# Attention scores on VectorE and ScalarE: one product per key unit, sums shared by two engines

## The chip, the cores and the metric

One core of a Trainium2 chip runs the whole program in one launch. The metric is the device time in microseconds; the kernel before has a median of 1359.05 us over three runs (1358.47 to 1362.22).

## The reference

Two equal layers in float32, for two sequences with one query token each. A layer is an attention block over a given cache and a gated feed-forward block, both with a LayerNorm ahead and a residual around:

```
x = x + A(layernorm(x)) ; x = x + B(layernorm(x))          # twice, with the same weights
A: q = x @ wq                    B=2, H=16 heads, Dh=256
   p = softmax(q . k_cache / 16) Sk=4096 keys for each head and sequence
   o = p @ v_cache, then o @ wo
B: h = relu(x @ W_gate) * (x @ W_up) ; h @ W_down          D=448, F=1792
```

The two caches are 2 x 16 x 4096 x 256 floats each, 134 MB a piece, and both layers read both of them.

## The kernel before

The caches go through SBUF in units. A unit is 1 MB: 128 partitions with 8 tiles (CT) of 256 floats (DH) each, so 1024 keys. One head of one sequence (a pair) is four units of K and four of V, and a layer has 32 pairs, which the text numbers u = 0 to 31. All loads are issued by SyncE (SP) at line 118, in an order fixed in advance: K of u, V of u - 1, after every odd u the head's weights (wq and wo, 896 KB), K of u + 1 and so on, at the end seven loads of W_gate and W_up (`w_in`) and four of W_down (`w_out`). Most K and V loads take four units in one transfer of 4 MB. The first thirteen loads of the second layer and the last twelve of each layer are single units.

The arena has room for 27 units: six blocks of four and three singles. A load is issued when the slot that it takes has been released (`release`, `pump`), and loads leave strictly in order. K of u + 3 takes the slots of K of u, so that its load waits for the scores of u; V goes likewise by the weighing.

The second layer goes through the pairs in reverse. The last pairs' units of the first layer stay in the arena for it (`keep`, `KEPT`): K of the second layer's u = 0, 1 and 2, V of its u = 0 and 1 and one unit of V of u = 2. While the feed-forward block runs between the layers, only what the few free slots hold can be loaded: K units 0 to 2 of u = 3 and two heads' weights. All later loads wait for scores: K unit 3 of u = 3 and the three V units of u = 2 take the slots of K of u = 0, the four K units of u = 4 those of K of u = 1, V of u = 3 the block of V of u = 0, and K of u = 5 the block of K of u = 2.

The function `score(u, c)` (lines 329 to 341) takes one K unit. For each of its eight tiles one VectorE instruction (line 336) multiplies the tile with the query, which stands alike in all 128 partitions, and sums the 256 products into one column of `s_of[u]`. The products are written over the tile, or into `junk` where the unit is kept for the second layer. The loop at line 433 sets the order of each engine's work for a pair u: unit 0 of the scores, `out_add` and `out_turn` for u - 2, units 1 and 2, `out_keep` and `project` for u - 2, in odd u `query` for the next head, `softmax_sum` for u - 1, unit 3, `softmax_max` and `softmax_exp` for u, then `weigh` for u - 1 on TensorE and `out_copy` for u - 1 on ScalarE. ScalarE's own work for a pair is small: the copy of the query (line 311, in odd u), two activations for the softmax (352 and 355) and the copy of the weighed sum (386). The schedule is written by hand; each engine executes its instructions in this order.

Of the kernel before, what the change touches and what calls it, by code (L numbers as in the profile page):

```python
# [9 lines left out]
AF = mybir.ActivationFunctionType  # L10
ALU = mybir.AluOpType
AX = mybir.AxisListType
RED = bass_isa.ReduceOp

B, D, H, S, DH, F = 2, 448, 16, 4096, 256, 1792
P = 128
# [3 lines left out]
CT = 8  # L20
# [5 lines left out]
SUMS = 96  # L26
SMALL = 13
ENDS = 12
HEAD = FULL * DH + P + 2 * D
EPS = 1e-5  # L30
SCALE = DH**-0.5
# [33 lines left out]
def two_layers(  # L65
# [10 lines left out]
    nc = tc.nc  # L76
# [45 lines left out]
    def get(*key):  # L122
        at = at_of[key]
        return arena[:, at * UNIT : (at + 1) * UNIT]

    def release(*key):
        units.free.add(at_of.pop(key))
        pump()
# [19 lines left out]
    def grouped(keys, begin, end):  # L148

        keys = list(keys)  # L150
        found, i = [], 0
        while i < len(keys):
            kind, name, c = keys[i]
            whole = kind in "kv" and c == 0 and begin <= i and i + NC <= len(keys) - end
            found.append((keys[i], NC if whole else 1))
            i += found[-1][1]
        return found
# [10 lines left out]
    of_second[NC - 1 : NC - 1] = heads  # L168
    pending += grouped(of_first, 0, ENDS) + [(key, 1) for key in ffn_loads]
    pending += grouped(of_second, SMALL, ENDS) + [(key, 1) for key in ffn_loads]  # L170

    row = consts.tile([P, 2 * DH], F32, name="row")
    junk = consts.tile([P, DH], F32, name="junk")
# [83 lines left out]
    def attention(order, after, begun):  # L257
# [4 lines left out]
        q_of, oT_of, s_of, mx_of, p_of, r_of, po_of, pT_of = ({} for _ in range(8))  # L262
# [3 lines left out]
        def query_of(u, pq):  # L266
            h, b = order[u]
            w = get("h", h, 0)
            for c in range(FULL):
                nc.tensor.matmul(  # L270
                    pq[:, b, :],
                    xT[:, c, b : b + 1].to_broadcast([P, P]),
                    w[:, c * DH : (c + 1) * DH],
                    start=(c == 0),
                    stop=False,
                )
            for j in range(2):
                nc.tensor.matmul(
                    pq[:, b, j * P : (j + 1) * P],
                    xT[:, FULL + j, b : b + 1].to_broadcast([P, P]),  # L280
                    w[:, FULL * DH : FULL * DH + P],
                    start=False,
                    stop=(j == 1),
                )
            q_of[u] = pq[:, b, :]
# [31 lines left out]
        def first_query():  # L317
# [3 lines left out]
            w = get("h", order[0][0], 0)  # L321
            for u, at in ((0, HEAD), (1, 0)):
                query_of(u, pq)
# [5 lines left out]
        def score(u, c):  # L329
            kt = get("k", order[u], c).rearrange("p (t n) -> p t n", t=CT)  # L330
            if c == 0:
                s_of[u] = work.tile([P, NT], F32, name="scores")
            kept = ("k", order[u], c) in after
            for t in range(CT):
                n = c * CT + t
                nc.vector.scalar_tensor_tensor(  # L336
                    junk if kept else kt[:, t, :], kt[:, t, :], 1.0, q_of[u],
                    op0=ALU.mult, op1=ALU.mult, accum_out=s_of[u][:, n : n + 1],
                )
            if not kept:  # L340
                release("k", order[u], c)

# [87 lines left out]
        ahead = 2 if ("k", order[0], 0) in keep else 0  # L430
        if ahead:
            query(ahead)
        for u in range(n_u + 2):
            if_pair(score, u, 0)
            if u == 0:
                inverse()
                nc.vector.tensor_scalar_mul(sr, rstd, SCALE)
                nc.vector.tensor_scalar_mul(nsr, rstd, -SCALE)
            if_pair(out_add, u - 2)
            if_pair(out_turn, u - 2)  # L440
            if_pair(score, u, 1)
            if_pair(score, u, 2)
            if_pair(out_keep, u - 2)
            if_pair(project, u - 2)
            if u % 2 and ahead < u + 1 < n_u:
                query(u + 1)
            if_pair(softmax_sum, u - 1)
            if_pair(score, u, 3)
            if_pair(softmax_max, u)
            if_pair(softmax_exp, u)  # L450
            for c in range(NC):
                if_pair(weigh, u - 1, c)
            if_pair(out_copy, u - 1)
# [87 lines left out]
    found = row[SUMS : SUMS + B, :D]  # L541
# [53 lines left out]
```

## Time and profile before

| | us |
|---|---|
| median of three runs | 1359.05 |
| the profiled execution, its own time | 1361.46 |
| its span in the profile | 1359.7 |
| VectorE busy | 796.3 (59%) |
| TensorE matmuls busy | 583.0 (43%) |
| ScalarE busy | 106.9 (8%) |

The profile is of one execution. It gives each engine's busy time, the share of time in which the core's 16 DMA engines were busy with the rate in GB/s, and chains of waits. Queue q1 carries the loads of SyncE. The queues q8 and q14 carry instructions, which the engines fetch while they run. The span falls into a first layer (to about 690 us), a stretch between the layers in which the load rate drops, and the second layer.

### The profile page before, as it was taken

Reading aid. Unit: us, or ns where it says so; the run is one execution under the profiler, and the core shown is the slowest. Engines: PE = TensorE matmul, PEld = TensorE weight load, DVE = VectorE, ACT = ScalarE, POOL = GpSimd, SP = SyncE. Lnnn points to the kernel's source line nnn. Section 1 sums busy time; section 2 is a strip of 40 time slices with the busy share of each in tenths; the row PEclk is TensorE's granted clock in tenths of the full one; section 3 lists DMA queues with packets and bytes.
Section 4 is the critical chain, followed back from the end, with each engine's and each line's share of the span. In section 5 each row is a group of like instructions: output and inputs, shape, how many; then the busy total and the mean of one; then the engine's idle time right before and its main releaser. Section 6 shows DMA issues by size and latency. Waiting matters only on the chain.

```text
span 1359.7 us, 11857 instructions
## 1 busy us (share of the span) xinstructions
PE 583.0 (43%) x3046; PEld 190.0 (14%) x3046; DVE 796.3 (59%) x4484; ACT 106.9 (8%) x314; POOL 76.6 (6%) x192
## 2 busy tenths in 40 slices
PE   2334335344244342443575444444244343443446
PEld 2111111111011110112131111111011110111112
DVE  4764664645646556466619984655646557456471
ACT  1100000000000000000011100000000000000001
POOL 0100000000000000000000100000000000000000
PEclk9666576666666756767676777666666665666667
DMA  9999999999999999999869999999999999999995
GB/s 397 438 427 429 432 428 431 431 430 431 429 429 431 429 434 430 429 428 425 328 259 370 417 433 431 430 428 428 431 428 436 434 427 427 431 429 433 425 416 194
DMA packets 29163, 563.33 MB, mean 414 GB/s; under 512 B 3236, under 2 KB 3240, under 8 KB 10024
## 3 DMA queue, kind: packets, MB, share of 16 engines
q1 hardware_dynamic: 29092, 562.58, 97.5%
q8 instruction: 24, 0.39, 0.1%
q14 instruction: 43, 0.35, 0.1%
q10 hardware_dynamic: 4, 0.00, 0.0%
HBM read 562.56 MB, written 0.00 MB: 414 GB/s over the span
## 4 chain that ended last, share of the span: by engine, by line
DVE 39%; DMA 34%; another core or an unknown queue 22%; PE 4%; issue 1%; ACT 0%; SPq 0%; DVEq 0%; POOL 0%; POOLq 0%; ACTq 0%
DVE arena L336 35%; DMA arena<-in_k_cache_dram 24%; DMA arena<-in_v_cache_dram 4%; DMA arena<-in_w_head_dram 3%; DMA arena<-in_w_in_dram 2%; DVE row L389 1%; DMA arena<-in_w_out_dram 1%; DVE ri L365 1%; PE po L375 1%; PE pf L518 1%; DVE mx L345 0%; PE acc L416 0%; PE pq L270 0%; PE pf L467 0%
## 5 line engine op out<-in xcount | busy, mean ns | idle before, releaser
L336 DVE SCALAR_TENSOR_TENSOR arena<-arena 128x256 f32<-128x256 f32 x1952 | 689.3, 421 | 453.6 <-DMA arena<-in_k_cache_dram 441.2
L375 PE MATMUL po<-arena,probs 128*2 128x512 f32 x2048 | 316.1, 764 | 176.2 <-DMA arena<-in_v_cache_dram 165.8
L397 PE MATMUL small<-ones,row 128*128 128x1 f32 x256 | 61.6, 344 | 369.5 <-DVE row L389 369.5
L336 DVE DVE_READ_ACCUMULATOR arena<-arena 128x1 f32 x1952 | 160.4, 82 | 0.0
L397 PEld LDWEIGHTS small<-ones,row 128*128 128x128 f32 x256 | 56.1, 305 | 431.6 <-DVE row L389 431.6
L416 PE MATMUL acc<-arena,oT 128*2 128x448 f32 x128 | 51.6, 905 | 142.1 <-DVE oT L406 142.1
L375 PEld LDWEIGHTS po<-arena,probs 128*2 128x2 f32 x2048 | 54.2, 98 | 388.4 <-issue 359.7
L299 PE MATMUL pq<-arena,xs 128*33 128x256 f32 x174 | 77.6, 616 | 60.3 <-DMA arena<-in_w_head_dram 60.3
L315 POOL PARTITION_BROADCAST arena<-arena x58 | 28.0, 552 | 635.6 <-ACT arena L311 623.5
L352 ACT ACTIVATE nm<-top,nsr 128x1 f32<-128x1 f32 x64 | 18.9, 295 | 528.5 <-POOL top L347 528.5
L347 POOL PARTITION_ALL_REDUCE top<-mx x64 | 24.5, 382 | 531.2 <-DVE mx L345 530.0
L311 ACT ACTIVATE arena<-pq 33x256 f32<-33x256 f32 x29 | 11.0, 378 | 515.7 <-PE pq L303 515.7
L389 DVE SCALAR_TENSOR_TENSOR row<-po,ri,row 128x256 f32<-128x256 f32 x64 | 30.7, 480 | 26.5 <-ACT row L386 26.4
L299 PEld LDWEIGHTS pq<-arena,xs 128*33 128x33 f32 x174 | 25.9, 165 | 130.7 <-issue 129.6
L386 ACT ACTIVATE row<-po,ri 128x256 f32<-128x256 f32 x64 | 30.2, 472 | 132.0 <-PE po L375 132.0
L336 DVE SCALAR_TENSOR_TENSOR junk<-arena,pq 128x256 f32<-128x256 f32 x64 | 26.9, 420 | 8.0 <-DMA arena<-in_k_cache_dram 6.0
L359 POOL PARTITION_ALL_REDUCE total<-rs x64 | 25.3, 395 | 64.3 <-ACT probs L355 64.3
L303 PE MATMUL pq<-arena,xs 128*33 128x128 f32 x116 | 28.3, 393 | 0.0
L355 ACT ACTIVATE probs<-scores,nm,sr 128x32 f32<-128x32 f32 x64 | 26.4, 413 | 2.1
L416 PEld LDWEIGHTS acc<-arena,oT 128*2 128x2 f32 x128 | 3.0, 82 | 144.8 <-DVE oT L406 144.8
L303 PEld LDWEIGHTS pq<-arena,xs 128*33 128x33 f32 x116 | 19.9, 171 | 15.3 <-issue 13.1
L467 PE MATMUL pf<-arena,xs 128*32 128x448 f32 x128 | 17.6, 698 | 3.1 <-DMA arena<-in_w_in_dram 2.3
(90 smaller groups left out, 187.6 us busy)
## 6 DMA issues: line engine op xcount, KB each, us to landing
arena<-in_k_cache_dram SPq DMA_DIRECT2D x57, 4096.0 KB, 50.4
arena<-in_v_cache_dram SPq DMA_DIRECT2D x57, 4096.0 KB, 54.3
arena<-in_w_head_dram SPq DMA_DIRECT2D x31, 896.0 KB, 43.2
arena<-in_v_cache_dram SPq DMA_DIRECT2D x19, 1024.0 KB, 21.0
arena<-in_k_cache_dram SPq DMA_DIRECT2D x16, 1024.0 KB, 25.4
arena<-in_w_in_dram SPq DMA_DIRECT2D x14, 896.0 KB, 18.3
arena<-in_w_out_dram SPq DMA_DIRECT2D x4, 896.0 KB, 16.7
arena<-in_w_out_dram SPq DMA_DIRECT2D x4, 672.0 KB, 9.9
```

The lines of the kernel that those rows point to most:

```text
L299: nc.tensor.matmul(q, xs[:, c, :], w[:, c * DH : (c + 1) * DH], start=(c == 0), stop=False)
L303: nc.tensor.matmul(q[:, j * P : (j + 1) * P], xs[:, FULL + j, :], w[:, FULL * DH : FULL * DH + P], start=False, stop=(j == 1),)
L315: nc.gpsimd.partition_broadcast(q_of[v], found[32 * b : 32 * b + 1], channels=P)
L336: nc.vector.scalar_tensor_tensor(junk if kept else kt[:, t, :], kt[:, t, :], 1.0, q_of[u], op0=ALU.mult, op1=ALU.mult, accum_out=s_of[u][: ...
L347: nc.gpsimd.partition_all_reduce(mx_of[u], mx, P, RED.max)
L355: nc.scalar.activation(p_of[u], s_of.pop(u), AF.Exp, bias=nm, scale=sr[:, b : b + 1], accum_out=rs)
L359: nc.gpsimd.partition_all_reduce(r_of[u], rs, P, RED.add)
L375: nc.tensor.matmul(po_of[u][32 * t : 32 * t + 2, :], p_of[u][:, n : n + 2], vt[:, 2 * t * DH : (2 * t + 2) * DH], start=(c == 0), stop=(c ...
L386: nc.scalar.activation(row[:, :DH], po_of[u][:, :DH], AF.Copy, scale=r_of[u][:, 0:1])
L389: nc.vector.scalar_tensor_tensor(row[:, :DH], po_of.pop(u)[:, DH:], r_of[u][:, 1:2], row[:, :DH], op0=ALU.mult, op1=ALU.add,)
L397: nc.tensor.matmul(pT_of[u][:, c : c + 1], row[:, c * P : (c + 1) * P], ones, start=True, stop=True,)
L416: nc.tensor.matmul(acc[at : at + B], oT_of[h][:, c, :], wo[:, c * D : (c + 1) * D], start=(n < 3), stop=(n >= n_u - 3),)
```

## The change

In `score`, units that are neither kept nor of the first two pairs of the first layer take another path. One `tensor_mul` multiplies the whole unit (2048 floats per partition) with the query, which is broadcast over the eight tiles. ScalarE then sums three tiles, each by an activation Copy with an accumulated output, and VectorE sums the other five by one `reduce_sum`. The products stand in place of the keys as before, and the unit is released when both engines are done. In the first layer this concerns 27 pairs (u = 2 to 28), in the second all 32. Everything else stays.

```diff
+BY_ACT = 3
...
-            for t in range(CT):
-                n = c * CT + t
-                nc.vector.scalar_tensor_tensor(
-                    junk if kept else kt[:, t, :], kt[:, t, :], 1.0, q_of[u],
-                    op0=ALU.mult, op1=ALU.mult, accum_out=s_of[u][:, n : n + 1],
-                )
+            found = s_of[u][:, c * CT : (c + 1) * CT]
+            if kept or ahead and u < ahead:
+                for t in range(CT):
+                    nc.vector.scalar_tensor_tensor(
+                        junk if kept else kt[:, t, :], kt[:, t, :], 1.0, q_of[u],
+                        op0=ALU.mult, op1=ALU.mult, accum_out=found[:, t : t + 1],
+                    )
+            else:
+
+                nc.vector.tensor_mul(kt, kt, q_of[u][:, None, :].to_broadcast([P, CT, DH]))
+                for t in range(BY_ACT):
+                    nc.scalar.activation(
+                        kt[:, t, :], kt[:, t, :], AF.Copy, accum_out=found[:, t : t + 1]
+                    )
+                nc.vector.reduce_sum(found[:, BY_ACT:], kt[:, BY_ACT:, :], axis=AX.X)
```

`ahead` is 2 in the first layer and 0 in the second.

## Rows read from the trace of the kernel before

**Rows 1.** The page, parts 1 to 3: engines, load rate, DMA queues.
```profile
PE 583.0 (43%) x3046; PEld 190.0 (14%) x3046; DVE 796.3 (59%) x4484; ACT 106.9 (8%) x314; POOL 76.6 (6%) x192
...
GB/s 397 438 427 429 432 428 431 431 430 431 429 429 431 429 434 430 429 428 425 328 259 370 417 433 431 430 428 428 431 428 436 434 427 427 431 429 433 425 416 194
...
q1 hardware_dynamic: 29092, 562.58, 97.5%
q8 instruction: 24, 0.39, 0.1%
q14 instruction: 43, 0.35, 0.1%
```

**Rows 2.** Stretches: busy us (instructions) by engine, last clock, DMA share, GB/s.
```profile
20.00:660.00 640.00, 260.72 (x1316) 85.33 (x1314) 385.22 (x2164) 47.70 (x142) 36.51 (x90) 0.65 1.00 429
676.00:688.00 12.00, 6.66 (x44) 3.29 (x48) 2.29 (x12) 2.39 (x4) 0.00 (x0) 0.84 0.08 35
750.00:752.00 2.00, 0.00 (x0) 0.00 (x0) 1.97 (x12) 0.68 (x3) 0.37 (x1) 1.00 0.65 279
752.00:1342.00 590.00, 250.15 (x1316) 77.58 (x1320) 352.81 (x2011) 44.89 (x137) 35.30 (x87) 0.66 1.00 427
1343.00:1354.00 11.00, 8.96 (x81) 2.75 (x73) 1.67 (x5) 1.13 (x4) 0.00 (x0) 1.00 0.07 28
```

**Rows 3.** Chain of waits through the layers' border: start, us, what.
```profile
658.97 20.86 DMA arena<-in_v_cache_dram
...
679.88 1.08 PE po L375 x8
...
714.80 2.85 DVE arena L336 x16
...
735.55 2.77 DVE arena L336 x16
```

**Rows 4.** Chain of waits at the end of the program.
```profile
1337.89 16.16 DMA arena<-in_w_out_dram
...
1354.10 0.99 PE pf L518 x6
```

**Rows 5.** SyncE's loads in order of issue, around the layers' border.
```profile
661.46 0.33 SPq L118 DMA_DIRECT2D arena<-in_w_in_dram  x1
...
664.11 8.74 SPq L118 DMA_DIRECT2D arena<-in_w_in_dram  x4
...
738.76 0.38 SPq L118 DMA_DIRECT2D arena<-in_v_cache_dram  x1
750.52 0.33 SPq L118 DMA_DIRECT2D arena<-in_k_cache_dram  x1
...
766.58 0.33 SPq L118 DMA_DIRECT2D arena<-in_k_cache_dram  x1
```

**Rows 6.** VectorE by line and shape: count, busy us, mean ns, idle before.
```profile
L336 DVE SCALAR_TENSOR_TENSOR arena<-arena 128x256 f32<-128x256 f32 x1952 | 689.3, 421 | 453.6 <-DMA arena<-in_k_cache_dram 441.2 <-ACT arena L324 7.6 <-POOL arena L315 4.7
L345 DVE TENSOR_REDUCE mx<-scores 128x1 f32<-128x32 f32 x64 | 11.9, 186 | 2.2
L490 DVE TENSOR_TENSOR row<-pf,row 128x448 f32<-128x448 f32 x2 | 1.2, 624 | 8.1 <-PE pf L467 8.1
L189 DVE TENSOR_REDUCE sel<-ident 128x2 f32<-128x128 f32 x1 | 0.3, 279 | 0.0
```

**Rows 7.** ScalarE in order of time: an accumulating copy.
```profile
1336.05 0.54 ACT L225 ACTIVATE row<-acc 96x448 f32<-96x448 f32 x1 [2.40 <-PE acc L416]
1336.49 0.19 ACT L225 ACTIVATION_READ_ACCUMULATOR row<-acc 96x1 f32 x1
```

**Rows 8.** The second layer's end in order of time: exponentials, TensorE.
```profile
1318.03 0.41 ACT L355 ACTIVATE probs<-scores,nm,sr 128x32 f32<-128x32 f32 x1
...
1324.18 1.04 PE L375 MATMUL po<-arena,probs 128*2 128x512 f32 x8
...
1331.39 1.71 PE L375 MATMUL po<-arena,probs 128*2 128x512 f32 x8 [0.57 <-DMA arena<-in_v_cache_dram]
```

## The prediction

> **What bounds the kernel now.** I read the page first: the loads run at 425 to 438 GB/s in nearly every slice, and only the slices at the start, at the layers' border (328, 259, 370) and at the end fall off; VectorE is busy in 59% [rows 1]. So inside a layer the loads decide, and VectorE has 453.6 us in which it waits, 441.2 of them for K [rows 6]. A slower or faster VectorE matters only where the loads wait for released slots.
>
> The chain of waits shows two such hinges. At the border TensorE waits for the first layer's last V load until 679.8, and from 714.80 on VectorE's score line is the chain itself [rows 3]. At the end the chain is the last `w_out` load, landing at 1354.06, and TensorE behind it [rows 4].
>
> The table of stretches then shows why loads land so late. From 676 to 688 the DMA share is 0.08 at 35 GB/s, from 1343 to 1354 it is 0.07 at 28 GB/s [rows 2]. One of 16 engines alone would be 0.0625: fifteen have run dry and one trails. A load has landed only when its last part has, so every wait in the program goes by this one. At the border it still has five `w_in` loads to carry when the V load lands [rows 5]; a sixteenth of 896 KB at its 27 GB/s is 2.1 us, so it ends at about 679.8 + 10.6 = 690.4, the others by about 676.1: 14.3 us behind. At the end it is 1354.1 - 1342.5 = 11.6 behind, though around 751 all had run dry together [rows 2].
>
> What does this engine carry that the others don't? Queues q8 and q14 fetch code. TensorE's 6092 instructions fit q8 (0.39 MB, 64 bytes each). At 64 bytes VectorE's 4484 are 0.287 of q14's 0.35 MB, some 35 of its 43 loads of 8 KB (128 instructions) [rows 1]. Charged to VectorE's code, the lag is 14.3 us over 2164 / 128 = 16.9 loads, 0.85 us each, in the first layer, and 11.6 over 2011 / 128 = 15.7, or 0.74, in the second [rows 2]. No row shows which engine carries which code: this is my reading.
>
> **The change, part by part.** *VectorE's time for a unit.* Now sixteen instructions take 2.77 us [rows 3], 346 ns a tile although one lasts 421 [rows 6]: they overlap. The product: 448 elements (one operand in PSUM) take 624 ns; the reductions of 32 and 128 columns, 186 and 279, give 0.97 ns an element [rows 6]. At 1.04 ns, which with the 421 ns leaves some 155 fixed, 2048 elements take 2.29. The reduction reads it, so there is no overlap: 0.04 of wait, then 1280 elements in 1.49, of which the next product hides 0.08. Sum 3.74, that is 0.97 more. From below: 3328 elements at 0.97 and 0.16 fixed, 3.39, plus 0.62; from above: no overlap, and ScalarE's end awaited each time, 4.1, plus 1.33.
>
> *ScalarE's part.* An accumulating copy of 448 columns with its read-out takes 1336.68 - 1336.05 = 0.63 [rows 7]; 256 columns should take 0.5, three 1.5, beside the reduction's 1.49. It ends 0.1 to 0.3 later, and only the release and `softmax_max` wait for that.
>
> *Inside a layer* nothing follows: 29 pairs in 590 us [rows 2] are 20.3 us a pair; VectorE works 12.2 of these and gets 3.9 more. If that cover were gone, each us over would cost 60 us in all. ScalarE's sums stand behind waits in its queue: unit 3 of odd u behind the copy of the next query, unit 0 behind the copy of the weighed sum. I put that at 2 to 3 us in odd u, inside the idle 4.
>
> *The restart of the second layer* is VectorE's. The load of K for u = 5 issues at 750.52 [rows 5], after twelve units of scores; the rate around it (279 GB/s) says that the queue was just empty [rows 2]. So its delay counts in full: 12 x 0.97 = 11.6, and 0.4 for ScalarE's tail in three softmax steps: **+12.0 us** (bounds +7.5 and +16). SyncE issues in order, so V for u = 4 and the next head come later as well; they bring 20 us of work, and K of u = 6, now at 766.58 [rows 5], moves to some 781, 2 us before that runs out.
>
> [...] The tile rate of 346 ns leaves only 80 ns a tile to save, less than the 1280 elements that are now read twice.
>
> *The trailing engine.* In a new unit VectorE has 2 instructions for 16, ScalarE 6 more. First layer: 2164 - 27 x 56 = 652, 5.1 loads, 4.3 us; ScalarE 142 + 27 x 24 = 790, 6.2 loads, 5.2 us. Second: 2011 - 29 x 56 = 387, 3.0 loads, 2.2 us; ScalarE 833, 6.5, 4.8. If each engine's code comes by a DMA engine of its own, the later of the two counts: the lag falls by 14.3 - 5.2 = **9.1** and 11.6 - 4.8 = **6.8 us**. I take this value because TensorE's q8, with as many bytes as q14, has left no second engine as far behind. If both ride on one engine, it falls by 14.3 - 9.6 = 4.7 and 11.6 - 7.0 = 4.6; if ScalarE's code delays no one, by 10.0 and 9.4.
>
> *The end.* The last two K loads' scores take 8 x 0.97 = 8 us more. The exponentials are done at 1318.5, TensorE takes up the last pair at 1324.18 and waits for its last V load at 1331.39 [rows 8]: covered by 5 us. That V load and the last `w_out` both come earlier with the lag, so TensorE's tail moves along.
>
> The sum, against the profiled execution: 1361.46 + 12.0 - 9.1 - 6.8 = 1357.6. The median of the runs shown is 2.4 lower than that execution: **1355.2 us**.
>
> **The rivals.** (1) *The lag stays.* One DMA engine is slower by itself, and less code changes nothing. For it: the trace names no engine for the code. Against it: the lag restarts from zero and then fits the code in both layers. Then only the restart counts: 1371.0, slower; it decides from a gain in lag under 8 us. [...]
> (2) *ScalarE's code rides on the same engine*: 12.0 - 9.3, so 1361.8.
> (3) *ScalarE's order holds the slots.* A sum behind the copy of a query or of a weighed sum releases K late while loads are short, and K of u = 6 misses its 2 us: 3 to 8 more, 1358 to 1363.
> (4) *The restart is cheaper* (+7.5: 1350.7) or ScalarE's code delays no one (12.0 - 19.4: 1351.8).
> (5) *The fixed cost decides*: without overlap a unit was 8 x 503 = 4.0 us (421 and 82 for the read-out of the sum) and gets 0.25 cheaper: -3 at the restart, 1340. The tile rate of 346 ns speaks against it [rows 3]. [...]
>
> **How the numbers follow.** Three runs of this kernel differ by 0.3%, about 4 us, and less can't be told from no change; so faster is below 1355.0, slower above 1363.1. Forecast 0.42 (1350 to 1360, half of it below 1355), (1) 0.17, (2) 0.12, (3) 0.11, (4) 0.13, (5) 0.05. Faster: 0.21 + 0.13 + 0.05 = 0.39. Slower: (1) 0.17 and a part of (2) and (3), 0.05: 0.22. No change: 0.39. The range, 1347 to 1369, leaves out (5) and half of (1); the forecast's own is 1350 to 1360.
>
> **What would show it.** Right: a product of about 2.29 us and a reduction of 1.45 by line; between 714 and 765 the K load of u = 5 twelve us later after its layer's first score; the stretch at 0.06 before the border shrunk from 12 us to some 3 and the one at the end from 11 to 5; fewer q14 loads (about 28). Wrong: the tail of 11 us still there; VectorE waiting for ScalarE within units; gaps in the load rate after 770, or inside a layer.

## The result and the profile after

The changed kernel takes 1340.34 us (median of four runs, 1338.35 to 1341.89) against 1360.63 in the same comparison: a ratio of 0.985, 95% interval 0.9825 to 0.9875, about 20 us faster. The forecast was 1355.2, in a range from 1347 to 1369. The direction came true, the size didn't: 1340 lies below the range.

One thing that both the section on the change and the prediction say is wrong. `ahead` is 2 in the *second* layer, whose first K is kept, and 0 in the first; I read it the other way round. So the new path runs in 29 pairs of the first layer (u = 0 to 28) and 30 of the second (u = 2 to 31), and the second layer's first two pairs keep the old one.

The page of the changed kernel, parts 1 to 3, beside [rows 1]:

```profile
PE 560.5 (42%) x3046; PEld 188.2 (14%) x3046; DVE 1012.3 (76%) x1180; ACT 407.1 (30%) x1730; POOL 107.1 (8%) x192
...
GB/s 400 431 434 429 432 425 434 431 433 428 427 433 431 433 428 430 428 436 423 419 329 365 382 423 435 433 431 430 427 434 432 427 431 433 427 432 431 434 415 298
...
q8 instruction: 24, 0.39, 0.1%
q14 instruction: 30, 0.25, 0.0%
```

VectorE works 216 us more and the program is faster. The rate inside the layers is unchanged (430 and 426 GB/s in the stretches below, 429 and 427 before); q14 has 30 loads of code for 43.

Its costliest new lines, by shape (count, busy us, mean ns):

```profile
L344 DVE TENSOR_TENSOR arena<-arena 128x2048 f32<-128x2048 f32 x236 | 539.3, 2285 | 152.6 <-DMA arena<-in_k_cache_dram 147.4 <-ACT arena L325 4.7 <-POOL top L357 0.6
L349 DVE TENSOR_REDUCE scores<-arena 128x5 f32<-128x1280 f32 x236 | 350.6, 1486 | 8.2
...
L355 DVE TENSOR_REDUCE mx<-scores 128x1 f32<-128x32 f32 x64 | 11.9, 186 | 69.5 <-ACT arena L346 66.0
```

The chain of waits at the layers' border and in the restart, beside [rows 3] (start, us, what):

```profile
646.41 19.81 DMA arena<-in_v_cache_dram
...
666.26 1.73 PE po L385 x8
...
701.09 2.85 DVE arena L338 x16
...
740.95 2.21 DVE arena L344
743.18 1.47 DVE scores L349
```

and SyncE's loads around the restart, beside [rows 5]; the first two are K for u = 5 and V for u = 4:

```profile
740.73 0.33 SPq L119 DMA_DIRECT2D arena<-in_k_cache_dram  x1
741.15 0.38 SPq L119 DMA_DIRECT2D arena<-in_v_cache_dram  x1
754.37 0.33 SPq L119 DMA_DIRECT2D arena<-in_w_head_dram  x1
761.08 0.33 SPq L119 DMA_DIRECT2D arena<-in_k_cache_dram  x1
```

Three differences of these times make up the whole change of the span (1359.7 to 1340.1, -19.6):

| stretch | before | after | difference |
|---|---|---|---|
| start to the second layer's first score | 714.80 | 701.09 | -13.7 |
| from there to the load of K for u = 5 | 35.72 | 39.64 | +3.9 |
| from there to the end | 609.2 | 599.4 | -9.8 |

Stretches of the changed kernel, in the columns of [rows 2]:

```profile
20.00:646.00 626.00, 245.37 (x1315) 82.68 (x1313) 489.36 (x530) 195.71 (x838) 46.29 (x90) 0.66 1.00 430
670.00:676.00 6.00, 4.62 (x21) 2.40 (x24) 1.79 (x11) 1.91 (x3) 0.00 (x0) 0.50 0.42 177
676.00:678.00 2.00, 2.00 (x16) 0.69 (x12) 0.00 (x0) 0.00 (x0) 0.00 (x0) 0.50 0.02 7
738.00:740.00 2.00, 0.00 (x0) 0.00 (x0) 1.97 (x2) 0.82 (x5) 0.00 (x0) 0.55 0.08 33
737.00:1328.00 591.00, 249.65 (x1352) 79.94 (x1356) 464.40 (x399) 194.70 (x842) 54.45 (x88) 0.66 1.00 426
1328.00:1334.00 6.00, 4.52 (x49) 1.60 (x41) 1.18 (x2) 0.43 (x2) 0.00 (x0) 1.00 0.41 170
```

The 12 us before the border in which one DMA engine of sixteen worked alone have become a fall-off of some 6 us, and by 676 to 678 nearly all have run dry; the 11 us before the end have shrunk likewise. At 738 to 740 the loads stand at 33 GB/s, waiting for VectorE's scores of u = 2.

### The profile page after: what moved, and what is told of

It is laid out like the page before. It is cut to its first block, busy times and chain, and to the rows that moved or that the text cites. A ratio compares the mean times of both kernels' runs of the same rounds, so it can differ in the third digit from the quotient of the medians.

```text
span 1340.1 us, 10126 instructions
## 1 busy us (share of the span) xinstructions
PE 560.5 (42%) x3046; PEld 188.2 (14%) x3046; DVE 1012.3 (76%) x1180; ACT 407.1 (30%) x1730; POOL 107.1 (8%) x192
## 4 chain that ended last, share of the span: by engine, by line
DMA 59%; DVE 29%; PE 8%; ACT 2%; issue 2%; POOL 0%; DVEq 0%; SPq 0%; POOLq 0%; ACTq 0%
DMA arena<-in_k_cache_dram 56%; DVE arena L344 16%; DVE scores L349 10%; DMA arena<-in_v_cache_dram 3%; PE pq L300 2%; DVE arena L338 2%; PE acc L426 2%; PE pf L477 1%; ACT arena L346 1%; DVE row L399 1%; DMA arena<-in_w_out_dram 1%; PE pq L304 1%; PE pq L271 0%; PE small L216 0%; PE pf L528 0%
## 5 line engine op out<-in xcount | busy, mean ns | idle before, releaser
L344 DVE TENSOR_TENSOR arena<-arena 128x2048 f32<-128x2048 f32 x236 | 539.3, 2285 | 152.6 <-DMA arena<-in_k_cache_dram 147.4
L346 ACT ACTIVATE arena<-arena 128x256 f32<-128x256 f32 x708 | 286.0, 405 | 539.8 <-DVE arena L344 539.8
L349 DVE TENSOR_REDUCE scores<-arena 128x5 f32<-128x1280 f32 x236 | 350.6, 1486 | 8.2
L385 PE MATMUL po<-arena,probs 128*2 128x512 f32 x2048 | 302.9, 739 | 128.9 <-DMA arena<-in_v_cache_dram 116.5
L346 ACT ACTIVATION_READ_ACCUMULATOR arena<-arena 128x1 f32 x708 | 132.4, 187 | 0.0
L357 POOL PARTITION_ALL_REDUCE top<-mx x64 | 49.4, 771 | 594.4 <-DVE mx L355 594.4
L300 PE MATMUL pq<-arena,xs 128*33 128x256 f32 x174 | 74.2, 593 | 11.7 <-DMA arena<-in_w_head_dram 11.7
L355 DVE TENSOR_REDUCE mx<-scores 128x1 f32<-128x32 f32 x64 | 11.9, 186 | 69.5 <-ACT arena L346 66.0
L312 ACT ACTIVATE arena<-pq 33x256 f32<-33x256 f32 x29 | 10.9, 376 | 140.8 <-PE pq L304 140.8
L300 PEld LDWEIGHTS pq<-arena,xs 128*33 128x33 f32 x174 | 25.3, 163 | 80.7 <-issue 79.1
```

Source lines behind the costliest of these rows:

```text
L300: nc.tensor.matmul(q, xs[:, c, :], w[:, c * DH : (c + 1) * DH], start=(c == 0), stop=False)
L344: nc.vector.tensor_mul(kt, kt, q_of[u][:, None, :].to_broadcast([P, CT, DH]))
L346: nc.scalar.activation(kt[:, t, :], kt[:, t, :], AF.Copy, accum_out=found[:, t : t + 1])
L349: nc.vector.reduce_sum(found[:, BY_ACT:], kt[:, BY_ACT:, :], axis=AX.X)
L357: nc.gpsimd.partition_all_reduce(mx_of[u], mx, P, RED.max)
L385: nc.tensor.matmul(po_of[u][32 * t : 32 * t + 2, :], p_of[u][:, n : n + 2], vt[:, 2 * t * DH : (2 * t + 2) * DH], start=(c == 0), stop=(c ...
```

## The experiments

Theory C is the prediction's: the code that VectorE fetches holds up one DMA engine, and every load lands when that one is done. Rival W: not the code but what VectorE's many short operations do in SBUF. The runs are called e1 to e4, f1 to f4 and g1 to g4, in the order in which they stand here. Ratios are to the kernel before, which took 1360.3 to 1361.1 us beside them.

**Empty instructions, first try.** In the kernel after, behind each new unit:

```diff
+                for _ in range(14):
+                    nc.vector.nop(nofuse=True)     # others: nc.gpsimd, nc.scalar, or 7 and 7
```

Expected with all 14 on VectorE: 

> Kernel after with 14 empty instructions on VectorE behind each new unit, as many as the change took away there (59 pairs x 4 x 14 = 3304, 25.8 loads of 128); nothing of the computation is altered. Theory C (VectorE's code makes one DMA engine trail): the lags come back, 13.7 us at the border and 9.8 in the second layer, so about 1340 + 20 = 1360, with q14 at about 56 loads and a stretch of some 11 us at a DMA share of 0.06 before the end. Rival W (what trails the DMA engine is VectorE's many short operations on SBUF, not the fetching of their code): the empty instructions read and write nothing, so 1340 +- 3.

On GpSimd: 

> Kernel after with the same 14 empty instructions for each new unit on GpSimd instead of VectorE. Theory C in its form 'each engine's code comes by a DMA engine of its own': GpSimd gets 13 loads in each layer, its DMA engine trails by some 10 to 12 us, so 1340 + 14 to 20 = 1354 to 1360. Theory C in the form 'only VectorE's code hurts': 1340 +- 3. Rival W: 1340 +- 3.

On ScalarE: 

> Kernel after with the same 14 empty instructions for each new unit on ScalarE, behind its three sums. ScalarE then has some 20 loads a layer for 7. Theory C, own DMA engine for each: it trails by 14 to 18 us, 1340 + 18 to 26 = 1358 to 1366. Only VectorE's code: 1340 +- 3, plus what the empty instructions delay in ScalarE's queue, under 2.

Half on VectorE, half on GpSimd: 

> Kernel after with 7 empty instructions on VectorE and 7 on GpSimd for each new unit: the same code in all as in the two runs with 14 on one engine. Theory C, own DMA engine for each: VectorE has 11 loads a layer and GpSimd 8, the worse lag is about 10 us for 4.5, so 1340 + 9 to 11 = about 1350. Both streams on one DMA engine, or a cost of code in general: as with 14 on one engine, about 1360. Rival W: 1340 +- 3.

Measured: 1340.16, 1341.14, 1340.49 and 1340.70 us, ratios of 0.9849 to 0.9855, like the changed kernel (0.985). But the spans hold 10126 instructions, exactly as many as after, and q14 has 30 or 31 loads: the empty instructions were left out when the program was built. So the runs decide nothing between C and W; they are four more measurements of the changed kernel.

**Code without work, on VectorE (f1).** Engine no-operations stay in the program. In the kernel before, where VectorE has room:

```diff
+            if u > 2 and not kept:
+                for _ in range(14):
+                    nc.vector.engine_nop()
             if not kept:
                 release("k", order[u], c)
```

> Kernel before with 14 engine no-operations on VectorE behind the scores of each unit (u from 3 on, not the kept ones: 220 units, 3080 instructions, 24 loads of 128). They read and write nothing; VectorE has the idle time for them. Theory C (VectorE's code makes one DMA engine trail): 11.4 loads more in the first layer at 13.7 / 12.7 = 1.08 us, 12.7 in the second at 9.8 / 13 = 0.75, so 1360.8 + 12.3 + 9.5 = about 1383, with some 67 loads in q14 and both stretches near a DMA share of 0.06 about twice as long. Rival W (VectorE's many short operations on SBUF disturb the transfers): 1361 +- 3, q14 up all the same.

Measured 1385.03 us, ratio 1.0182 (1.0167 to 1.0198): +24.7 us. On the page the code has come (43 loads before); no-operations have no count of their own there:

```profile
q14 instruction: 67, 0.55, 0.1%
```

The chain at the border, and the two stretches with one DMA engine at work:

```profile
670.12 20.09 DMA arena<-in_v_cache_dram
690.25 1.58 PE po L378 x8
```

```profile
688.00:700.00 12.00, 8.11 (x44) 3.59 (x40) 2.28 (x12) 2.39 (x4) 0.00 (x0) 0.61 0.06 27
1366.00:1376.00 10.00, 8.09 (x69) 2.53 (x65) 1.67 (x5) 1.13 (x4) 0.00 (x0) 0.98 0.07 29
```

The V load lands 10.4 us later than in [rows 3] and the end comes later still. Code that reads and writes nothing does this, so W is not needed for it. One part missed: the two stretches are no longer than before. The rate shows why, falling ahead of them (321 and 293 GB/s in the slices at the border): with loads landing so late, slots come free late and the other fifteen engines are held up too.

```profile
GB/s 397 437 432 427 430 431 427 434 428 430 430 430 429 430 431 430 429 430 321 293 284 368 420 429 429 431 432 431 430 429 429 431 430 431 428 431 429 403 293 183
```

**The same time without the code (f2).**

```diff
+            if u > 2 and not kept:
+                nc.vector.memset(kt[:, :4, :], 0.0)
```

> Kernel before with one memset of 1024 columns on VectorE behind the scores of each of the same 220 units: about the working time of the 14 no-operations (0.9 us), 220 instructions for 3080. What is overwritten has been read. Theory C: 1.7 loads more, 1361 + 1 to 2. A theory by which VectorE's working time or its late release of K sets the loads back: the same rise as with the 14 no-operations.

Measured 1362.53 us, ratio 1.0016 (1.0006 to 1.0025): +2.2. VectorE works 179 us longer than before and two more loads of code come:

```profile
PE 562.3 (41%) x3046; PEld 188.1 (14%) x3046; DVE 975.2 (72%) x4704; ACT 104.1 (8%) x314; POOL 77.5 (6%) x192
...
q14 instruction: 45, 0.37, 0.1%
```

The work that was put in is longer than that of the no-operations, 0.81 us a unit for 0.17 (not 0.9, as I had expected), so the control errs to the safe side: working time and a late release are not the cause.

**The same code on another engine (f3, f4).** In the kernel before as above with `nc.gpsimd.engine_nop()`, and in the kernel after behind each new unit.

Before: 

> Kernel before with the 14 engine no-operations on GpSimd for the same 220 units: 24 loads more for GpSimd, 12 a layer, VectorE's code as before. Theory C with a DMA engine of its own for each engine's code: GpSimd's trails by about as much as VectorE's already does, and the later one counts: 1361 + 0 to 3. Theory C with one DMA engine for all of q14: as for VectorE, about 1383. Rival W: 1361 +- 3.

After: 

> Kernel after with 14 engine no-operations on GpSimd for each new unit (236 units, 3304 instructions, 25.8 loads). Theory C with a DMA engine of its own for each engine's code: GpSimd's becomes the one that trails, by 12 to 13 loads a layer in place of the 4 to 5 us left, so 1340.5 + 14 to 18 = 1354 to 1359. Theory C with one DMA engine for all of q14: 26 loads on top of 30, 1340.5 + 20 to 25. Only VectorE's code hurts, or rival W: 1340.5 +- 3.

Measured 1360.44 us, ratio 1.0000 (0.9991 to 1.0010), for the first: 24 loads more and nothing lost, where the same loads for VectorE cost 24.7 us. And 1348.98 us, ratio 0.9922 (0.9907 to 0.9937), for the second: 8.6 us lost of the 20.3 gained, less than expected. Their q14 rows, in this order:

```profile
q14 instruction: 67, 0.55, 0.1%
```

```profile
q14 instruction: 56, 0.46, 0.1%
```

So the cost is not that of code in general, nor of one DMA engine for all of q14: as long as VectorE's code trails more, GpSimd's is free; where VectorE's is short, GpSimd's shows. At the border of this last run the V load lands 4.4 us later than after:

```profile
650.85 19.81 DMA arena<-in_v_cache_dram
```

**What the single transfers say.** The traces also hold each transfer and the landing of each of a load's sixteen parts, which the page of the profile does not show, and there the trailing engine can be seen directly. In the trace before, 31 loads of code take 0.32 to 0.34 us, and behind 26 of them a 32 KB data transfer starts at once that takes 1.88 us, where such transfers mostly take 1.21 to 1.22. The 0.32 and the 0.66 that the next takes longer are 0.98 us of delay for a load of code. In f1 there are 53 loads of this kind, in f3 31 as before, after the change 8, so they are VectorE's. GpSimd's new loads in f3 mostly take 0.31 us with 1.57 us behind them, which is 0.66 of delay, and ScalarE's after the change 0.31 with 1.59, or 0.69. The largest lag of a load's last part behind its eighth, in each layer (of 152 of the 202 loads, whose parts can be told apart):

| run | first layer, us | second layer, us |
|---|---|---|
| before | 17.3 | 13.4 |
| after | 4.7 | 3.9 |
| f1, more code for VectorE | 28.4 | 26.5 |
| f2, more work for VectorE | 18.7 | 15.4 |
| f3, before with more code for GpSimd | 16.3 | 13.6 |
| f4, after with more code for GpSimd | 8.8 | 7.7 |

Before, the last part falls back alone, mostly in steps of 0.8 to 1.0 us through the first layer: it is one DMA engine that carries VectorE's code. The 16.9 loads that [rows 2] give the first layer make 16.6 us at 0.98, so little is left there for W. In f3 the last part is at most 8.8 us behind the fifteenth, though 16.3 behind the eighth: there a second engine trails too, GpSimd's. In f1 the lag has shrunk again before the border, to 13.0 us behind the fifteenth part, as the other engines ran out of slots; so the stretches there are no longer than before. The change takes 12.6 and 9.5 us off the lag, for 13.7 and 9.8 gained.

**The restart (g1, g2).** Where the new path begins in the second layer, in the kernel after:

```diff
-            if kept or ahead and u < ahead:
+            if kept:                              # from u = 0
+            if kept or ahead and u < 3:           # from u = 3
```

From 0: 

> Kernel after with the new path in the second layer's pairs u = 0 and 1 too, which is what the prediction had taken the change to do. By the price from the traces (0.98 us for a unit on VectorE, in full at the restart): 8 x 0.98 = 7.8, and 0.3 for ScalarE's tail in two softmax steps, less 112 VectorE instructions a layer (-0.5): 1340.5 + 7.6 = 1348. If loads are not short at the restart, or the longer score of a unit is hidden there: 1340.5 +- 2.

From 3: 

> Kernel after with the old path in the second layer's pair u = 2 as well, so that the load of K for u = 5 waits for old scores alone. By the same price: -3.9, 1336.5; VectorE's 56 more instructions are less than half a load. If another wait (head weights, the block of V) follows at once behind K of u = 5: 1338 to 1340.5.

Measured 1348.84 us, ratio 0.9915 (0.9900 to 0.9930), and **1336.42 us, ratio 0.9822 (0.9805 to 0.9840)**, faster than both kernels. The first scores stand at

```profile
701.41 2.30 DVE arena L344
```

```profile
699.88 2.85 DVE arena L338 x16
```

and K for u = 5 is issued at

```profile
748.35 0.33 SPq L119 DMA_DIRECT2D arena<-in_k_cache_dram  x1
```

```profile
735.61 0.33 SPq L119 DMA_DIRECT2D arena<-in_k_cache_dram  x1
```

That is 46.94 and 35.73 us after the first score, against 39.64 after and 35.72 before. The 0, 4 and 12 new units ahead of that load cost 0, 3.9 and 11.2 us, and the totals follow: 1336.4, 1340.3, 1348.8.

**One layer at a time (g3, g4).**

```diff
-            if kept or ahead and u < ahead:
+            if kept or order is second:                 # first layer only
+            if kept or order is first or u < ahead:     # second layer only
```

> Kernel after with the new path in the first layer only (29 pairs); the second as before. Theory C: the first layer's V load lands 13.7 us earlier as in the trace after, the rest stays: 1360.3 - 13.7 = 1346.6. If the gain had come from the end of the program: 1358 to 1361.

> Kernel after with the new path in the second layer only (30 pairs). Theory C: restart +3.9, second layer -9.8: 1360.3 - 5.9 = 1354.4; the border stays where it was before (first score of the second layer at about 714.8).

Measured 1347.62 us, ratio 0.9905 (0.9890 to 0.9920), and 1354.13 us, ratio 0.9954 (0.9939 to 0.9969): 13.5 and 7.0 us gained, in sum 20.4, the whole. The second layer's first score, from the chains of the two in this order:

```profile
698.86 2.85 DVE arena L338 x16
```

```profile
713.56 2.85 DVE arena L338 x16
```

## Why the prediction was right in its mechanism and wrong in its size

*What bounds the kernel.* Right. One DMA engine trails because of VectorE's code, and the loads land with it; f1 to f3 show it from both sides, 24.7 us for 24.1 loads of VectorE's code and none for as many of GpSimd's, and the lags in the table follow.

*VectorE's time for a unit.* Right: a product of 2285 ns and a reduction of 1486 (2.29 and 1.49 were worked out), one unit each 3.72 us where it is bound, for 3.74. The 1.04 ns an element stands in no row as it is: [rows 6] give 0.97 by the reductions and (624 - 421) / (448 - 256) = 1.06 by L490 and the old instruction. The changed kernel shows it, (2285 - 421) / (2048 - 256) = 1.04.

*ScalarE's part.* A little less than worked out: the three sums of a unit take 1.30 us (739.18 to 740.48) for 1.5, and end 0.19 us ahead of the reduction, not 0.1 to 0.3 behind it, where nothing stands before them in ScalarE's queue.

*Inside a layer.* Right. VectorE waits 66.0 us for ScalarE at `softmax_max` (L355), 2.1 on average for each odd u, and nothing follows: the rate inside the layers is 430 and 426 GB/s, for 429 and 427 in [rows 2].

*The restart, +12.0 us.* This step failed, by the misreading of `ahead`. Twelve units were charged where four are new, and the restart cost 3.9 us. The price itself held: g1, which is the kernel that the prediction had in mind, issues K for u = 5 11.2 us later.

*The trailing engine, -9.1 and -6.8 us.* This step failed in its size: -13.7 and -9.8. Three terms were off. The first layer lost the code of 29 pairs, not 27: 12.7 loads. The price of a load was taken as 0.85 and 0.74 us, from lags that had shrunk by the time they were read (the last part is 16.5 us behind the fifteenth at 670 us, 13.7 at 690.7), since the other engines had been waiting for slots; the transfers show 0.98, and f1 has 24.7 / 24.1 = 1.03 for the whole program. And ScalarE's new loads were charged at VectorE's price and set the floor, 5.2 and 4.8 us; they cost 0.69 each, or 4.5 in each layer for some 6.5 loads, about as much as the 4 that VectorE's own code still causes. The choice between one DMA engine and two was right: on a single one these would add up to 8.5, and after the change no load's last part is more than 4.7 us behind its eighth. By these prices the two lags fall by 12.0 and 10.9 us, in sum 22.9, for 23.5 measured.

With the pairs read rightly and my own prices the sum would have been 1361.46 + 4.1 - 8.7 - 6.8 - 2.4 = 1347.7, so that about half of the miss is the misreading and half the prices of the loads. Both erred the same way.

*The end.* Right that TensorE's tail moves along. It now runs without a wait for `w_out`, beside [rows 4]:

```profile
1332.08 3.42 PE pf L528 x28
```

and takes up its last V load at 1311.67, beside [rows 8]:

```profile
1311.67 1.04 PE L385 MATMUL po<-arena,probs 128*2 128x512 f32 x8 [0.90 <-DMA arena<-in_v_cache_dram]
```

From that load to the end it is 28.4 us, for 28.3 before: what the program gains is that V load's.

*The rivals.* (1), a lag that stays, falls with f1 and with the result. (2), ScalarE's code on the same engine as VectorE's, has no run of its own (e3 was to be one); the lag of at most 4.7 us speaks against it, as said. (3) had nothing to act on: K of u = 6 is issued at 761.08, and the loads before it were still running (400 GB/s from 760 to 764). (4), 1351.8, came nearer than the forecast, in its part on ScalarE's code, which costs less than was charged. (5) names the measured time, 1340, and by luck: it wants a unit that gets cheaper, and the unit went from 2.77 to 3.72 us.

## What to carry to other kernels

Where loads set the time, look at the share of DMA time just before each stretch in which all stand still. Here it was 0.08 for 12 us and 0.07 for 11, near 1/16, because one engine trailed; VectorE's code was the cause, and fewer, longer instructions gained 20 us although VectorE worked 216 us more. Count the time saved only up to the next hinge, here the restart of the second layer, and use the slower form only where its engine has the idle time. And before a change is priced, each condition in it is to be worked through for both callers.

## What the runs showed of the hardware

A load of 128 instructions (8 KB) delayed its DMA engine by 0.98 us for VectorE, 0.69 for ScalarE and 0.66 for GpSimd, with data loads running at 426 to 430 GB/s. The larger part is in the data transfer behind it, for VectorE 1.88 us for 1.21; why that one takes longer is not shown.

GpSimd's maximum over partitions got slower beside the product. Its line after and before (ns: shortest, median, longest):

```profile
L357 POOL PARTITION_ALL_REDUCE top<-mx x64: 350/351/2322, 39.2 to 1303.7; - x64
```

```profile
L347 POOL PARTITION_ALL_REDUCE top<-mx x64: 350/352/482, 34.6 to 1317.3; - x64
```

The longest, 2322 ns, is about the product's 2285; before, the longest was 482, with an old instruction of 421 ns under way beside it. After the change 14 of the 64 take 1.95 to 2.32 us. Beside each of these a product runs that started before it, and each ends 0.21 to 0.24 us behind that product; the other 50, with no product beside them, take 0.35 to 0.37. What holds the 14 up is not shown. The exponentials of these pairs start up to 2 us later (2.32 less 0.35); whether a load was ever delayed by it was not measured.
